# A chunked attention with a token-mixing MLP on one core: mixed product on the full array, small weights on another queue, early casts and a new order of units

## The chip, the core and the metric

The kernel runs on one core of one Trainium2 chip. The metric is the device time of one execution in microseconds (us). Every comparison below is made with runs of the kernel before on the same chip, in the same rounds. A ratio is the mean time of one kernel's fast runs over that of the other's fast runs of the same rounds, so it is not quite the ratio of the medians that are quoted beside it. The span in a profile is some 1.8 us shorter than the time of the same execution.

## The reference

```
attention: q, k, v are [8, 8, 576, 64]; chunks of 64 tokens, no mixing between chunks
  scores = q_c @ k_c.T / 8;  attn = softmax(scores);  out = attn @ v_c
x = heads side by side                       # [8, 576, 512]
wq = x @ w_q;  wk = x @ w_k                  # [8, 576, 64] each
W  = (wq @ wk.T) / 8                         # [8, 576, 576]
out = relu(W @ x) @ w_out                    # [8, 576, 512]
```

Because (wq @ wk.T) @ x = wq @ (wk.T @ x), the kernel never forms W. It computes G = wk.T @ x, 64 x 512 per batch, and then the mixed product wq @ G.

## The kernel before

All work is cut into units and issued in the order of a list, PLAN. TensorE executes its share strictly in the order of the list. The digits are the unit's number and the batch; behind the colon stand the PSUM banks (the tile `banks`, into which TensorE writes).

- `Tq0b`, `Tk0b` (the first 6 of 9 row groups) and `Tq1b`, `Tk1b` (the other 3): VectorE transposes queries and keys.
- `S0b` (double) and `S2b` (single): scores on TensorE, exponentials on ScalarE.
- `Ahb`: attend for two heads on TensorE, normalization (0.21 + 0.82 us) on VectorE.
- `Xnb`: transposes of the result on TensorE, a copy on VectorE.
- `Qb`, `Kb`, `Gb`: projections, transposed key projection, G, each with a copy on ScalarE.
- `Mnb`: mixed product, relu on ScalarE. `O`, `P`: one or two output tiles. An output tile needs only old data, so it is the filler of the order.

```
PLAN = """
Tq00 Tk00 S00:02 Tk10 Tq10 A00:4 S20:0 Tq01 A30:2 Tk01 A20:0 A10:4 S01:62 Tk11 X00:0
X10:2 A01:4 Tq11 A11:0 Q0:2 S21:4 X01:0 Tq02 K0:6 A21:2 G0:0 M00:4 Tk02 A31:0 M10:2
M20:6 S02:42 Tq12 M30:6 X11:0 O:4 Q1:2 Tk12 O:0 ...            (cut)
"""
    load(0)
    make_identity(nc, ident[:])
    for n, w in enumerate((moe_w_q, moe_w_k)):
        for u in range(2):
            nc.gpsimd.dma_start(wraw[...], w...)              # float32 in memory, float16 in SBUF
    for b in range(1, VB):
        load(b)                                                # all loads on the GpSimd queue
...
    def mlp_w(b, a):                                           # Q; in batch 0 it casts wqk first
        ...                                                    # wq in partitions 0-63, wk in 64-127
        nc.scalar.copy(wT[b % 2][:, 0:S]..., a[:, :, 0:HS])
        nc.scalar.copy(wq2[b % 2][CH:, :]..., a[0:CH, :, 0:HS])   # wq again, in partitions 64-127
    def mlp_g(b, a):
        ...
        nc.scalar.copy(g16[b % 2][:], a[:, 0 : DM // 2])       # half of G in each 64 partitions
    def mix(b, n, a):
        i, half = n % 2, n // 2
        for h in range(2):                                     # K = 64: two row halves of the array
            nc.tensor.matmul(a[:, h, 0:HS],
                lhsT=g16[b % 2][CH * h : CH * h + CH, i * P : i * P + P],
                rhs=(wT, wq2)[h][b % 2][CH * h : CH * h + CH, half * HS : half * HS + HS], ...)
        nc.scalar.activation(..., AF.Relu, scale=scale_moe)
```

The softmax here doesn't subtract the row's maximum and nothing guards it: scores larger than these inputs give would overflow.

Of the kernel before, what the change touches and what calls it, by code (L numbers as in the profile page):

```python
# [10 lines left out]
F16 = mybir.dt.float16  # L11
F32 = mybir.dt.float32
# [3 lines left out]
PSUM = bass.MemoryType.PSUM  # L16

PLAN = """
Tq00 Tk00 S00:02 Tk10 Tq10 A00:4 S20:0 Tq01 A30:2 Tk01 A20:0 A10:4 S01:62 Tk11 X00:0
X10:2 A01:4 Tq11 A11:0 Q0:2 S21:4 X01:0 Tq02 K0:6 A21:2 G0:0 M00:4 Tk02 A31:0 M10:2  # L20
M20:6 S02:42 Tq12 M30:6 X11:0 O:4 Q1:2 Tk12 O:0 A02:6 K1:1 S22:4 A12:2 G1:0 M01:6 M11:4
M21:2 Tq03 Tk03 P:0 X02:4 Tk13 S03:26 A22:0 O:4 Tq13 A32:2 O:5 A03:0 M31:6 X12:2 A13:4
S23:6 Q2:0 Tq04 A23:2 O:4 K2:5 Tk04 O:6 A33:0 G2:2 S04:46 Tk14 X03:2 X13:0 O:4 Tq14
A04:2 M02:6 M12:0 Q3:4 A14:6 S24:0 Tq05 K3:2 O:3 M22:4 M32:0 A24:6 G3:2 Tk05 O:3 A34:0
M03:4 O:2 S05:46 Tq15 Tk15 X04:0 O:2 X14:4 M13:6 M23:0 S25:2 A05:4 M33:6 Q4:0 A25:2
A35:4 O:6 Tq06 K4:0 Tk06 Tq16 P:2 O:0 G4:1 A15:2 S06:46 X15:0 O:2 M04:4 Tk16 M14:0 X05:6
A06:2 S26:4 A16:0 O:6 A36:2 M24:4 M34:0 Q5:6 Tq07 X06:2 O:0 K5:1 Tk07 O:4 A26:2 Tq17
Tk17 G5:0 S07:64 O:1 X16:2 S27:6 M05:4 M15:0 Q6:2 A37:6 A27:4 O:0 K6:1 O:6 A17:2 G6:0
A07:4 M25:6 M35:0 X17:2 M06:6 X07:4 M16:0 M26:2 O:6 Q7:0 O:2 O:3 K7:0 O:1 M36:4 G7:2 O:0
M07:4 M17:1 M27:6 O:3 M37:4 O:0 O:1 O:2 O:0 O:1 O:2  # L30
"""


# [1 line left out]
def kernel(  # L35
# [10 lines left out]
    nc = tc.nc  # L46
    B, H, S, D = q.shape
    DM = moe_w_out.shape[0]
    DH = moe_w_q.shape[1]
    P = 128  # L50
# [21 lines left out]
    def each(n, shape, dt, name):  # L72
        return [sb.tile(shape, dt, name=f"{name}{i}") for i in range(n)]
# [2 lines left out]
    kn = each(B, [P, NT, R * D], F16, "kn")  # L76
    vt = each(VB, [P, NP, W], F16, "vt")
    wqk = sb.tile([P, NI, 2 * DH], F16, name="wqk")
    wraw = sb.tile([P, 2, NI, DH], F16, name="wraw")
    wout = sb.tile([P, NI, DM], F16, name="wout")  # L80
    ident = sb.tile([P, P], F16, name="ident")
    zero = sb.tile([P, 512], F16, name="zero")
# [7 lines left out]
    xt = [each(2, [P, S], F32, f"xt{i}_") for i in range(2)]  # L90
    identw = sb.tile([P, P], F32, name="identw")
    wT = each(2, [P, NJ * P], F16, "wT")
    wq2 = each(2, [P, S], F16, "wq2")
    wkn = each(2, [P, NJ, DH], F16, "wkn")
    g16 = each(2, [P, DM // 2], F16, "g16")
    rmx = each(2, [P, NI, 2 * S], F16, "rmx")
    spare = each(2, [P, 2 * DM], F32, "spare")
    mark = sb.tile([1, 2], F16, name="mark")
# [52 lines left out]
        clear_v(i, i > 0)  # L151
    load(0)
    make_identity(nc, ident[:])
    for n, w in enumerate((moe_w_q, moe_w_k)):
        for u in range(2):
            nc.gpsimd.dma_start(
                wraw[CH * u : CH * u + CH, n].rearrange("p (h e) j -> p h (e j)", e=2),
                w.rearrange("(u h p e) j -> u p h (e j)", u=2, h=2, e=2)[u],
            )
# [2 lines left out]

    for i in range(2):
        nc.vector.memset(wT[i][:, S:], 0.0)
    nc.vector.memset(padl[:], 1.0 / P)
    nc.vector.memset(padr[:], 0.0)
    nc.vector.memset(padr[:, 2 * D :], 1.0)
# [30 lines left out]
    def scores(b, s, slots):  # L198
        for t in range(TS):
            for ch in range(2):  # L200
                for e in range(2):
                    for n, a in enumerate(slots):
                        for i in range(2):
                            for u in range(2):
                                h = CH * (u ^ (s + n > 0))
                                o = (2 * t + ch) * CH
                                x = (b, TS * (s + n) + t, 2 * u + i, ch, e)
                                nc.tensor.matmul(  # L208
                                    a[h : h + CH, i, o : o + CH],
                                    lhsT=k_of(*x),  # L210
                                    rhs=q_of(*x),
                                    start=(e == 0),
                                    stop=(e == 1),
                                )
        for n, a in enumerate(slots):
            nc.scalar.activation(  # L216
                est[b % 2][s + n].rearrange("p i t c -> p i (t c)"),
                a[:, :, 0 : 2 * TS * CH],
                AF.Exp,
                scale=scale_attn,  # L220
            )

    def attend(b, h, a):
        af = a.rearrange("p i c -> p (i c)")
# [26 lines left out]

    def xtr(b, n, a):
        tx = a.rearrange("p i c -> p (i c)")
        if "ident" not in done:
            done["ident"] = 1
            nc.scalar.copy(identw[:], ident[:])  # L256
        for j in range(NJ):
            nc.tensor.transpose(  # L258
                tx[:, j * P : j * P + P],
                xn[b % 2].bitcast(F32)[:, j, n * P : n * P + P],  # L260
                identw[:],
            )
        nc.vector.tensor_copy(xt[b % 2][n][:], tx[:, 0:S])  # L263

    def mlp_w(b, a):
        if b == 0:
            nc.scalar.copy(
                wqk.rearrange("p i (n j) -> p n i j", n=2),
                wraw[:],
            )  # L270
        for i in range(NI):
            for h in range(2):
                nc.tensor.matmul(  # L273
                    a[:, h, 0:HS],
                    lhsT=wqk[:, i, :],
                    rhs=xt[b % 2][i // 2]
                    .bitcast(F16)
                    .rearrange("p (s e) -> p s e", e=2)[:, h * HS : h * HS + HS, i % 2],
                    start=(i == 0),
                    stop=(i == NI - 1),  # L280
                )
        nc.scalar.copy(  # L282
            wT[b % 2][:, 0:S].rearrange("p (h n) -> p h n", h=2), a[:, :, 0:HS]
        )
        nc.scalar.copy(
            wq2[b % 2][CH:, :].rearrange("p (h n) -> p h n", h=2), a[0:CH, :, 0:HS]
        )

    def mlp_k(b, a):
# [13 lines left out]
    def mlp_g(b, a):  # L303
        for j in range(NJ):
            for h in range(2):
                nc.tensor.matmul(  # L306
                    a[CH * h : CH * h + CH, 0 : DM // 2],
                    lhsT=wkn[b % 2][:, j, :],
                    rhs=xn[b % 2][:, j, h * 256 : h * 256 + 256],
                    start=(j == 0),  # L310
                    stop=(j == NJ - 1),
                )
        nc.scalar.copy(g16[b % 2][:], a[:, 0 : DM // 2])

    done = {"out": 0, "home": 0}

    def mix(b, n, a):
        i, half = n % 2, n // 2
        for h in range(2):
            nc.tensor.matmul(  # L320
                a[:, h, 0:HS],
                lhsT=g16[b % 2][CH * h : CH * h + CH, i * P : i * P + P],
                rhs=(wT, wq2)[h][b % 2][CH * h : CH * h + CH, half * HS : half * HS + HS],
                start=True,
                stop=True,
            )
        o = (b % 2) * S + half * HS
        nc.scalar.activation(  # L328
            rmx[(b // 2) % 2].rearrange("p (h i) n -> p i h n", h=2)[:, i, :, o : o + HS],
            a[:, :, 0:HS],  # L330
            AF.Relu,
            scale=scale_moe,
        )
# [99 lines left out]
```

## Time and profile before

| | before |
|---|---|
| time, median of 4 runs | 125.7 us (125.18 to 126.4) |
| span of the profile | 125.8 us (of a slow run, 127.58 us) |
| TensorE, VectorE, ScalarE busy | 100.6, 76.2, 81.9 us |
| granted TensorE clock, mean | 0.919 |

Three groups of the profile's view by lines that the change touches follow. The columns are line, engine, operation, output<-input, shapes and count; then busy us and mean ns of one; then the engine's idle time just before them, and what ended most of it.

```profile
L320 PE MATMUL banks<-wq,g 64*128 64x288 f16 x32 | 7.4, 290 | 0.0
...
L285 ACT CAST wq<-banks 64x576 f16<-64x576 f32 x8 | 5.0, 630 | 0.2
...
L313 ACT CAST g<-banks 128x256 f16<-128x256 f32 x8 | 3.0, 379 | 2.3 <-PE banks L306 2.1
```

The change takes the middle group away and doubles the last one in number.

### The profile page before, as it was taken

Reading aid. Unit: us, or ns where it says so; the run is one execution under the profiler, and the core shown is the slowest. Engines: PE = TensorE matmul, PEld = TensorE weight load, DVE = VectorE, ACT = ScalarE, POOL = GpSimd, SP = SyncE. Lnnn points to the kernel's source line nnn. Section 1 sums busy time; section 2 is a strip of 40 time slices with the busy share of each in tenths; the row PEclk is TensorE's granted clock in tenths of the full one; section 3 lists DMA queues with packets and bytes.
Section 4 is the critical chain, followed back from the end, with each engine's and each line's share of the span. In section 5 each row is a group of like instructions: output and inputs, shape, how many; then the busy total and the mean of one; then the engine's idle time right before and its main releaser. Section 6 shows DMA issues by size and latency. Waiting matters only on the chain. (4 is left out here: it accounts for less than half of the span.)

```text
span 125.8 us, 4598 instructions
## 1 busy us (share of the span) xinstructions
PE 100.6 (80%) x1958; PEld 61.5 (49%) x1958; DVE 76.2 (61%) x138; ACT 81.9 (65%) x137; POOL 72.0 (57%) x107
## 2 busy tenths in 40 slices
PE   6923450399779789989599979999999896999970
PEld 2303450385455645656556556565667564544420
DVE  5538319847794397979477955895999266400000
ACT  7992500512668777665569858668696795788960
POOL 6989889972798579579769948976400000000000
PEclk9996555556999999999999999999999999999999
DMA  1999999999999999999999999999999999936494
GB/s 13 161 172 160 140 172 176 150 145 196 195 163 170 190 158 139 175 190 153 160 190 162 155 183 181 129 168 186 167 214 386 366 348 382 376 122 244 167 352 150
DMA packets 63113, 24.55 MB, mean 195 GB/s; under 512 B 39540, under 2 KB 58484, under 8 KB 63092
## 3 DMA queue, kind: packets, MB, share of 16 engines
q0 software_dynamic: 57936, 14.82, 128.3%
q1 hardware_dynamic: 5156, 9.44, 20.2%
q8 instruction: 15, 0.25, 0.8%
q14 instruction: 6, 0.05, 0.1%
HBM read 29.62 MB, written 9.44 MB: 310 GB/s over the span
## 5 line engine op out<-in xcount | busy, mean ns | idle before, releaser
L341 PE MATMUL banks<-wout,rmx 128*128 128x512 f16 x144 | 35.7, 380 | 0.8 <-issue 0.8
L216 ACT ACTIVATE est<-banks 128x768 f16<-128x768 f32 x24 | 18.7, 809 | 19.1 <-PE banks L208 19.1
L118 POOL DMA_DIRECT2D vt<-in_v_dram x32 | 27.3, 859 | 6.0 <-DMA kn<-in_k_dram 1.7
L244 DVE TENSOR_TENSOR xn<-banks,rec 128x640 f16<-128x640 f32 x32 | 26.4, 824 | 1.1
L107 POOL DMA_DIRECT2D kn<-in_k_dram x32 | 20.9, 666 | 10.3 <-DMA vt<-in_v_dram 8.2
L208 PE MATMUL banks<-qT,kT 32*64 32x64 f16 x1152 | 14.6, 218 | 11.6 <-DVE rec L243 5.3
L107 POOL DMA_DIRECT2D qn<-in_q_dram x32 | 21.0, 680 | 1.0 <-POOLq L417 0.8
L328 ACT ACTIVATE rmx<-banks 128x576 f16<-128x576 f32 x32 | 19.5, 656 | 2.9 <-PE banks L320 2.6
L181 DVE STREAM_TRANSPOSE kT<-kn 128x768 f32<-128x768 f32 (+1 forms) x16 | 19.4, 1213 | 2.3 <-DMA kn<-in_k_dram 2.2
L208 PEld LDWEIGHTS <-kT 32*64 32x64 f16 x1152 | 12.1, 112 | 15.8 <-DVE rec L243 6.7
L341 PEld LDWEIGHTS <-rmx 128*128 128x128 f16 x144 | 12.5, 98 | 12.9 <-issue 1.1
L234 PE MATMUL banks<-vt,est 128*64 128x130 f16 x288 | 16.0, 241 | 3.4 <-DMA vt<-in_v_dram 2.4
L263 DVE COPY xt<-banks 128x576 f32<-128x576 f32 x16 | 12.0, 756 | 10.9 <-PE banks L258 9.2
L234 PEld LDWEIGHTS <-est 128*64 128x64 f16 x288 | 11.4, 120 | 9.9 <-issue 5.3
L181 DVE STREAM_TRANSPOSE qT<-qn 128x768 f32<-128x768 f32 (+1 forms) x16 | 12.4, 773 | 5.1 <-DMA qn<-in_q_dram 5.0
L258 PE MATMUL banks<-identw,xn 128*128 128x128 f32 x80 | 12.6, 298 | 3.4 <-ACT identw L256 1.8
L243 DVE RECIPROCAL rec<-banks 128x10 f32<-128x10 f32 x32 | 6.6, 206 | 11.5 <-PE banks L234 5.9
L258 PEld LDWEIGHTS banks<-identw,xn 128*128 128x128 f32 x80 | 9.7, 151 | 6.2 <-ACT identw L256 1.9
L359 ACT COPY qn<-banks 128x512 f32<-128x512 f32 x16 | 9.4, 590 | 4.6 <-PE banks L341 4.4
L359 ACT COPY kn<-banks 128x512 f32<-128x512 f32 (+1 forms) x15 | 9.2, 624 | 3.6 <-PE banks L341 3.2
L273 PE MATMUL banks<-xt,wqk 128*128 128x288 f16 x64 | 10.4, 309 | 0.0
L282 ACT CAST wT<-banks 128x576 f16<-128x576 f32 x8 | 5.1, 641 | 6.7 <-DVE xn L244 5.2
(36 smaller groups left out, 88.5 us busy)
## 6 DMA issues: line engine op xcount, KB each, us to landing
out_dram<-qn SPq DMA_DIRECT2D x16, 256.0 KB, 4.0
out_dram<-kn SPq DMA_DIRECT2D x14, 256.0 KB, 3.9
qn<-in_q_dram POOLq DMA_DIRECT2D x16, 192.0 KB, 6.1
kn<-in_k_dram POOLq DMA_DIRECT2D x16, 192.0 KB, 7.0
vt<-in_v_dram POOLq DMA_DIRECT2D x16, 192.0 KB, 6.2
qn<-in_q_dram POOLq DMA_DIRECT2D x16, 96.0 KB, 7.1
kn<-in_k_dram POOLq DMA_DIRECT2D x16, 96.0 KB, 5.6
vt<-in_v_dram POOLq DMA_DIRECT2D x16, 96.0 KB, 5.5
```

The source lines that it names most:

```text
L107: nc.gpsimd.dma_start(dst[b][CH * u : CH * u + CH, a:e, :], src[b] .rearrange("h s d -> (h s) d") .rearrange("(u t p r) d -> u p t (r d)", ...
L118: nc.gpsimd.dma_start(vt[b % VB][h : h + CH, a:e, D * u : D * u + D], v[b] .rearrange("h s d -> (h s) d") .rearrange("(u g p) d -> u p g d ...
L181: nc.vector.transpose(out=o, in_=src[b].bitcast(F32)[:, a:e, :].rearrange("p t (r d) -> p t r d", d=32),)
L208: nc.tensor.matmul(a[h : h + CH, i, o : o + CH], lhsT=k_of(*x), rhs=q_of(*x), start=(e == 0), stop=(e == 1),)
L216: nc.scalar.activation(est[b % 2][s + n].rearrange("p i t c -> p i (t c)"), a[:, :, 0 : 2 * TS * CH], AF.Exp, scale=scale_attn,)
L234: nc.tensor.matmul(af[CH * (c % 2) : CH * (c % 2) + CH, o : o + W], lhsT=lhsT, rhs=rhs, start=True, stop=True,)
L244: nc.vector.tensor_tensor(out=xn[b % 2] .rearrange("p j (a u b d) -> p j a u b d", a=2, u=2, b=2)[:, :, h // 2, :, h % 2, :], in0=xv[:, :, ...
L258: nc.tensor.transpose(tx[:, j * P : j * P + P], xn[b % 2].bitcast(F32)[:, j, n * P : n * P + P], identw[:],)
L263: nc.vector.tensor_copy(xt[b % 2][n][:], tx[:, 0:S])
L328: nc.scalar.activation(rmx[(b // 2) % 2].rearrange("p (h i) n -> p i h n", h=2)[:, i, :, o : o + HS], a[:, :, 0:HS], AF.Relu, scale=scale_moe,
L341: nc.tensor.matmul(a[:, x, :], lhsT=rmx[pr % 2][:, i, tl * P : tl * P + P], rhs=wout[:, 2 * (i % 2) + i // 2, :], start=(i == 0), stop=(i ...
L359: nc.scalar.copy(os_, a[:, 0:w, :])
```

## The change

G is kept whole in 64 partitions and padded with zeros to 128, so that the mixed product uses the full array and needs no second copy of wq. The small weights leave the GpSimd queue, so that batch 1 can be issued sooner. The casts move forward into idle time of ScalarE. The order of units is new, with S0 and S2 of a batch further apart.

```diff
 PLAN = """
-Tq00 Tk00 S00:02 Tk10 Tq10 A00:4 S20:0 Tq01 A30:2 Tk01 A20:0 A10:4 S01:62 Tk11 X00:0
-X10:2 A01:4 Tq11 A11:0 Q0:2 S21:4 X01:0 Tq02 K0:6 A21:2 G0:0 M00:4 Tk02 A31:0 M10:2
-M20:6 S02:42 ...                                                     (cut)
+Tk00 Tq00 Tq10 Tk10 Tq01 S00:02 S20:4 Tk01 A30:0 S01:24 A20:0 A00:6 Tk11 A10:2 X10:4
+Tq11 A11:0 A01:2 S21:4 X00:0 A31:2 Tq02 Tk02 Q0:4 A21:0 K0:2 Tq12 X01:4 S02:62 X11:0
+G0:6 ...                                                             (cut)
-    wraw = sb.tile([P, 2, NI, DH], F16, name="wraw")
+    wraw = sb.tile([P, 2, NI, DH], F32, name="wraw")
-    g16 = each(2, [P, DM // 2], F16, "g16")
+    g16 = each(2, [P, DM], F16, "g16")                # rows 64-127 are set to zero once
+    nc.sync.dma_start(mark[:], kn[0][P - 1 : P, 0, 0:2])   # waits for the first keys
-            nc.gpsimd.dma_start(wraw ...
+            nc.sync.dma_start(wraw ...
     def scores(b, s, slots):  ...
+        if b == 0 and s == 0:                          # both casts, taken out of X and Q
+            nc.scalar.copy(identw[:], ident[:])
+            nc.scalar.copy(wqk..., wraw[:])
-        nc.scalar.copy(wq2[b % 2][CH:, :]..., a[0:CH, :, 0:HS])
-        nc.scalar.copy(g16[b % 2][:], a[:, 0 : DM // 2])
+        for h in range(2):
+            nc.scalar.copy(g16[b % 2][0:CH, h * 256 : h * 256 + 256], a[CH * h : CH * h + CH, 0 : DM // 2])
-                lhsT=g16[b % 2][CH * h : CH * h + CH, i * P : i * P + P],
-                rhs=(wT, wq2)[h][b % 2][CH * h : CH * h + CH, half * HS : half * HS + HS],
+                lhsT=g16[b % 2][:, h * 256 + i * P : h * 256 + i * P + P],
+                rhs=wT[b % 2][:, half * HS : half * HS + HS],
```

More of the change, by code (lines that the diff above doesn't have):

```diff
@@ L18 @@
 PLAN = """
-Tq00 Tk00 S00:02 Tk10 Tq10 A00:4 S20:0 Tq01 A30:2 Tk01 A20:0 A10:4 S01:62 Tk11 X00:0
-X10:2 A01:4 Tq11 A11:0 Q0:2 S21:4 X01:0 Tq02 K0:6 A21:2 G0:0 M00:4 Tk02 A31:0 M10:2
-M20:6 S02:42 Tq12 M30:6 X11:0 O:4 Q1:2 Tk12 O:0 A02:6 K1:1 S22:4 A12:2 G1:0 M01:6 M11:4
-M21:2 Tq03 Tk03 P:0 X02:4 Tk13 S03:26 A22:0 O:4 Tq13 A32:2 O:5 A03:0 M31:6 X12:2 A13:4
-S23:6 Q2:0 Tq04 A23:2 O:4 K2:5 Tk04 O:6 A33:0 G2:2 S04:46 Tk14 X03:2 X13:0 O:4 Tq14
-A04:2 M02:6 M12:0 Q3:4 A14:6 S24:0 Tq05 K3:2 O:3 M22:4 M32:0 A24:6 G3:2 Tk05 O:3 A34:0
-M03:4 O:2 S05:46 Tq15 Tk15 X04:0 O:2 X14:4 M13:6 M23:0 S25:2 A05:4 M33:6 Q4:0 A25:2
-A35:4 O:6 Tq06 K4:0 Tk06 Tq16 P:2 O:0 G4:1 A15:2 S06:46 X15:0 O:2 M04:4 Tk16 M14:0 X05:6
-A06:2 S26:4 A16:0 O:6 A36:2 M24:4 M34:0 Q5:6 Tq07 X06:2 O:0 K5:1 Tk07 O:4 A26:2 Tq17
-Tk17 G5:0 S07:64 O:1 X16:2 S27:6 M05:4 M15:0 Q6:2 A37:6 A27:4 O:0 K6:1 O:6 A17:2 G6:0
-A07:4 M25:6 M35:0 X17:2 M06:6 X07:4 M16:0 M26:2 O:6 Q7:0 O:2 O:3 K7:0 O:1 M36:4 G7:2 O:0
-M07:4 M17:1 M27:6 O:3 M37:4 O:0 O:1 O:2 O:0 O:1 O:2
+Tk00 Tq00 Tq10 Tk10 Tq01 S00:02 S20:4 Tk01 A30:0 S01:24 A20:0 A00:6 Tk11 A10:2 X10:4
+Tq11 A11:0 A01:2 S21:4 X00:0 A31:2 Tq02 Tk02 Q0:4 A21:0 K0:2 Tq12 X01:4 S02:62 X11:0
+G0:6 Tk12 A02:4 Q1:2 M00:0 S22:6 M10:4 K1:2 A12:0 A32:6 A22:4 G1:0 Tk03 Tq03 O:1 M20:6
+M30:2 M01:4 M11:0 O:6 X12:2 X02:4 Tq13 S03:06 O:2 Tk13 Q2:4 A03:0 S23:6 A13:4 K2:2 M21:0
+M31:6 O:3 Tq04 G2:0 A33:4 A23:6 O:1 M02:2 Tk04 M12:4 Tq14 O:0 M22:6 O:1 Tk14 M32:2 X13:4
+X03:6 S24:0 S04:24 Q3:6 O:0 A24:2 A14:4 A34:6 K3:1 O:0 O:1 Tq05 Tq15 G3:2 A04:4 O:0 O:1
+M03:6 Tk15 M13:4 Tk05 X14:2 M23:0 X04:6 O:4 M33:0 S25:2 S05:64 Tq06 Q4:0 P:2 A25:0 A15:4
+K4:6 O:7 A05:0 G4:2 A35:4 O:3 Tk16 X05:0 M04:4 O:2 Tq16 M14:6 X15:4 S26:0 Tk06 M24:2
+Q5:6 A36:0 S06:24 Tq07 O:6 K5:0 Tk07 M34:2 O:1 A06:4 A16:6 G5:0 A26:2 O:1 M05:4 O:0
+X06:6 M15:2 Tk17 S07:40 X16:6 O:2 M25:4 Q6:6 Tq17 S27:0 A17:4 A07:6 K6:2 O:3 M35:0 A27:4
+G6:2 A37:6 O:3 X07:0 M06:4 X17:6 O:2 M16:0 Q7:4 O:2 K7:0 M26:4 O:1 G7:0 M36:4 O:1 M07:6
+M17:2 O:0 M27:4 M37:6 O:1 O:0 O:2 O:1 O:0 O:2
 """
@@ L92 @@
     wT = each(2, [P, NJ * P], F16, "wT")
-    wq2 = each(2, [P, S], F16, "wq2")
     wkn = each(2, [P, NJ, DH], F16, "wkn")
-    g16 = each(2, [P, DM // 2], F16, "g16")
+    g16 = each(2, [P, DM], F16, "g16")
     rmx = each(2, [P, NI, 2 * S], F16, "rmx")
@@ L153 @@
     make_identity(nc, ident[:])
+    nc.sync.dma_start(mark[:], kn[0][P - 1 : P, 0, 0:2])
     for n, w in enumerate((moe_w_q, moe_w_k)):
         for u in range(2):
-            nc.gpsimd.dma_start(
+            nc.sync.dma_start(
                 wraw[CH * u : CH * u + CH, n].rearrange("p (h e) j -> p h (e j)", e=2),
@@ L164 @@
         nc.vector.memset(wT[i][:, S:], 0.0)
+        nc.vector.memset(g16[i][CH:, :], 0.0)
     nc.vector.memset(padl[:], 1.0 / P)
@@ L221, in scores @@
             )
+        if b == 0 and s == 0:
+            nc.scalar.copy(identw[:], ident[:])
+            nc.scalar.copy(
+                wqk.rearrange("p i (n j) -> p n i j", n=2),
+                wraw[:],
+            )
     def attend(b, h, a):
@@ L253, in xtr @@
         tx = a.rearrange("p i c -> p (i c)")
-        if "ident" not in done:
-            done["ident"] = 1
-            nc.scalar.copy(identw[:], ident[:])
         for j in range(NJ):
@@ L265, in mlp_w @@
     def mlp_w(b, a):
-        if b == 0:
-            nc.scalar.copy(
-                wqk.rearrange("p i (n j) -> p n i j", n=2),
-                wraw[:],
-            )
         for i in range(NI):
@@ L283, in mlp_w @@
             wT[b % 2][:, 0:S].rearrange("p (h n) -> p h n", h=2), a[:, :, 0:HS]
-        )
-        nc.scalar.copy(
-            wq2[b % 2][CH:, :].rearrange("p (h n) -> p h n", h=2), a[0:CH, :, 0:HS]
         )
@@ L312, in mlp_g @@
                 )
-        nc.scalar.copy(g16[b % 2][:], a[:, 0 : DM // 2])
+        for h in range(2):
+            nc.scalar.copy(
+                g16[b % 2][0:CH, h * 256 : h * 256 + 256],
+                a[CH * h : CH * h + CH, 0 : DM // 2],
+            )
     done = {"out": 0, "home": 0}
```

## The prediction

> **What bounds the kernel now.** I began with the busy table by stretches of time, because one average over the span mixes a start that waits with an end that is full. Its columns are the stretch and its length, then busy us (with instruction counts) of PE, PEld, DVE, ACT and POOL, the granted clock, the DMA share and GB/s.
>
> ```profile
> 11.00:25.00 14.00, 5.44 (x280) 4.68 (x280) 8.30 (x13) 4.04 (x7) 13.26 (x21) 0.50 1.82 159
> 25.00:30.00 5.00, 4.96 (x36) 3.90 (x37) 3.15 (x7) 0.50 (x1) 2.86 (x5) 0.50 1.51 163
> 30.00:36.30 6.30, 4.57 (x97) 2.85 (x95) 4.87 (x7) 4.30 (x8) 4.51 (x6) 0.94 1.59 188
> 36.30:47.60 11.30, 10.12 (x225) 6.55 (x226) 7.28 (x10) 8.38 (x15) 8.60 (x13) 1.00 1.86 169
> ...
> 95.40:109.10 13.70, 12.07 (x254) 7.70 (x253) 8.18 (x14) 10.00 (x18) 0.00 (x0) 1.00 1.00 370
> 109.10:122.00 12.90, 12.76 (x78) 5.74 (x76) 0.00 (x0) 10.93 (x22) 0.00 (x0) 1.00 0.61 229
> ```
>
> There are three regimes. Up to about 30 us TensorE is mostly idle and at half clock. From 36 to 109 it is busy some 90% of the time. In the last 13 us it is full. So the end is set by when TensorE gets going, by what it has to do, and by the holes in between. Loads end near 90 us and don't set the end: the last batch's first query part was issued at 79.36 and its transpose ran at 91.74 without a wait for data.
>
> Next the timeline of the start (start, duration, engine, what, and in brackets the idle time before it and what ended it):
>
> ```profile
> 18.55 0.98 DVE L181 STREAM_TRANSPOSE qT<-qn 128x768 f32<-128x768 f32 x1 [3.48 <-DMA qn<-in_q_dram]
> ...
> 20.62 1.53 DVE L181 STREAM_TRANSPOSE kT<-kn 128x768 f32<-128x768 f32 x1
> ...
> 22.20 1.08 PE L208 MATMUL banks<-qT,kT 32*64 32x64 f16 x96 [4.43 <-DVE rec L243]
> ...
> 25.04 2.39 PE L258 MATMUL banks<-identw,xn 128*128 128x128 f32 x10 [1.76 <-ACT identw L256]
> ```
>
> VectorE waited 3.48 us for the queries of batch 1; from 18.55 to 30.7 it then worked with only some 2 us of holes, and TensorE followed it (the 4.43 us wait ends when the key transpose ends at 22.15). The cast of the identity, last in ScalarE's order, held the transposes another 1.76 us. This stretch is bound by that arrival and by VectorE's order.
>
> Last, the mixed product among its neighbours on TensorE (same columns):
>
> ```profile
> 85.73 1.03 PE L341 MATMUL banks<-wout,rmx 128*128 128x512 f16 x4
> 86.69 0.29 PE L320 MATMUL banks<-wT,g 64*128 64x288 f16 x1
> 86.69 0.29 PE L320 MATMUL banks<-wq,g 64*128 64x288 f16 x1
> 86.82 0.28 PE L320 MATMUL banks<-wT,g 64*128 64x288 f16 x1
> 86.82 0.28 PE L320 MATMUL banks<-wq,g 64*128 64x288 f16 x1
> 87.04 0.77 PE L258 MATMUL banks<-identw,xn 128*128 128x128 f32 x5
> ```
>
> The two halves start together, and the next pair comes 0.13 us later: a unit M costs 0.125 us, not 0.25. But the four output matmuls before it need 4 x 0.216 = 0.86 us, and M starts 0.96 us after they did; the last pair takes 0.22 until the transposes start. So about 0.10 us is lost on entering and again on leaving the half-array shape. The same shows at other changes of shape (attend to output at 89.17: 0.10 more than attend to attend), and not between two full-array kinds (output at 108.25, projection at 109.12: 0.87).
>
> **What the Trainium skill says.** "TensorEngine Tiling (Array Packing)", section Key Properties: changing the tiling mode drains TensorE. The trace agrees, at about 0.10 us a change. "TensorE: Matmul & The Clock Gate", Part 3 (packing small matmuls): matmuls in different row groups run concurrently; agrees, both at 86.69. The same page, Part 1: the clock starts at half rate and is released after some 3.4 us of activity; agrees roughly, as the clock is 0.50 from 11 to 30 us and full after the dense stretch from 25 on. "DMA: Bandwidth & Descriptors", Issuing engines are not separate DMA queues: all queues share the same 16 engines, so another queue saves only issue time. No run here shows that yet; the moved weights test it.
>
> **The change part by part.**
>
> *Full-array mix.* Each M goes from 0.125 to 2 x 0.12 = 0.245 us: 32 x 0.12 = +3.84 us of streaming. Against this, M no longer changes the shape next to transposes, projections, key products and outputs. I counted changes of shape along both orders (four kinds: full, 128x64 for A and G, 32x64 for S, 64x128 for the old M): 93 before, 55 after. So -38 x 0.10 = -3.8 us. The full array in the old order would have 71 changes, 3.84 - 2.2 = +1.6 us: the order pays the rest.
>
> TensorE's sum at full clock, from start-to-start distances in the timeline (0.85 a double S, 0.52 a single, 0.31 A, 0.54 X, 1.0 Q, 0.15 K, 0.55 G, 0.865 an output tile): 8x0.85 + 8x0.52 + 32x0.31 + 16x0.54 + 8x1.0 + 8x0.15 + 8x0.55 + 36x0.865 = 74.3. Before: + 32x0.125 + 93x0.10 = 87.6. After: + 32x0.245 + 55x0.10 = 87.6. TensorE's work is unchanged; this surprised me, as the streaming alone looked like a loss.
>
> *ScalarE.* Eight copies into the second half are gone: 8 x 0.630 (row of wq) = -5.0. The copy of G (0.379) becomes two of 64 partitions; halving partitions saved nothing for wq against wT (0.630 against 0.641), so + 8 x 0.38 = +3.0. Net -2.0 us on an engine that is busy 65%: nearly all beside other work. The key copy comes 0.63 sooner and the second half of G 0.38 later, worth 0.25 us where the chain Q-K-G-M has no filler. The output units fill most of it: I count 0.2 us.
>
> *Early casts.* The identity cast (0.30) and weight cast (0.63) move from 24.68 to about 15, when ScalarE is idle. This removes the 1.76 us wait, but VectorE's order is the bound behind it, so I give it no separate credit. The weights are now float32 on the sync queue behind the first keys (landed 9.33); if late, they delay the exponential of S20, for which there are some 3 us of room.
>
> *Weights off the GpSimd queue.* Four issues of 0.60 us go: batch 1 is issued 2.4 us sooner. The transfers still share the engines, busy over 90% from 3 us on, so I expect the queries of batch 1 not 2.4 but about 1 us sooner: 17.5 instead of 18.55.
>
> *Order at the start.* The new order moves attend 0 of batch 0 out of VectorE's idle time (14 to 15 us, 1.04 us) and leaves X01 (0.76) for later. The first keys are transposed before the first queries, so S00 starts after 9.33 + 1.53 + 0.98 = 11.8 instead of 10.9, with no effect, because batch 1 isn't there yet. From Tq01 to Tk02 VectorE has four transposes of b1 (0.98+1.53+0.87+0.57), seven attends (7 x 1.04), two copies (2 x 0.76), Tq02 and Tk02 (0.98+1.55): 15.3 us. From 17.5, with 1.5 to 2 us of holes, S02 starts at about 34.5 to 35 against 36.33, having had 9.2 us of TensorE work before it against 10.3. TensorE's lag behind its own sum thus goes from 26.0 to about 25 to 25.5: a gain of 0.8 us.
>
> *Order in the middle.* The lag before is 26.0 at S02, 31.9 at S07 (95.42 - 63.5), 34.3 at the end (121.88 - 87.6). Of these 8.3 us, some 3.8 are holes inside units (0.65 at 43.1, 0.55 at 56.1, 1.26 at 61.5, 0.75 at 74.8, 0.63 in two others) that wait for no engine; an order can't remove them. About 3 are waits for VectorE or ScalarE (1.24 at 106.27, 0.85 at 36.33, 0.47 at 44.7, 0.42 at 85.16). With S0 and S2 of a batch apart, I expect a third of these back: 1.0 us, a choice rather than a result.
>
> Sum: 0.0 (TensorE) - 0.8 (start) - 1.0 (middle) - 0.2 (chain) = -2.0 us. The tail after TensorE (a copy of 0.58 and the last transfer, 3.9 us together) stays. From 125.5 that is 123.5 us.
>
> **Rivals.** (1) *The full array costs what it streams.* If the 0.10 at a shape change is not really saved, TensorE has +3.8 us; as it is full at the end, the time would be near 127. For it: M is denser in the last third, where nothing hides it. Against it: the gaps around the old M are in every case I looked at.
> (2) *Loads take over.* If batches are started sooner but the engines can't deliver, VectorE waits for each batch and only the last one's slack counts. For it: the DMA row is 9 to slice 34 and loads go at 160 to 170 GB/s. Against it: batches 2 to 6 had 2.8 to 6 us between estimated landing and transpose. It would leave 125 to 126.
> (3) *The order removes most waits*, and the denser start brings the full clock 2 us sooner. Then 3 us of waits and 1 to 2 us at half clock come back: 121 to 122. Against it: some waits always return in another place, and VectorE bounds the start.
>
> **Range and chances.** My sum is 123.5, with rival 3 somewhat likelier than rival 1 because the new order looks made to group full-array work. I put 123.4, with 121.0 to 126.0 as the range. The bound for "faster by over 2%" is 122.98, a little below my number: 0.40. Slower by over 2% (127.98) needs rival 1 in full: 0.05. The rest, 0.55, is within 2%.
>
> **What would show it.** Right: M pairs 0.12 apart, one after another, with the next full-array unit following without a gap; TensorE's busy sum within 2 us of 100.6; Tq01 near 17.5; S02 near 35 and S07 between 93 and 96; ScalarE near 80. Wrong: waits for q or k before the transposes of batches 2 to 7 (rival 2); a last stretch after S07 longer than before's 26.5 us (rival 1); a new wait of ScalarE for the weights near 14 us that delays S20; or a clock that reaches 1.0 well before or after 30 us.

## The result

The changed kernel took 129.73 us in the median of 4 runs (128.49 to 130.09), against 125.7 us before. Executions over 1.5% slower than the fastest of the same kernel are left out of the means. The ratio of the fast runs is 1.0299, with a 95% interval of 1.021 to 1.039: slower by 3%, where 1.7% faster was predicted. Its profile is of a fast run: span 128.3 us, clock 0.894, TensorE, VectorE and ScalarE busy 101.4, 75.7 and 79.3 us. So the work is as predicted and the time isn't.

The busy table by equal stretches tells where the time went. Its columns are the stretch and its length, busy us (with instruction counts) of PE, PEld, DVE, ACT and POOL, the clock, the DMA share and GB/s. First the control, which is the kernel before in a fast run:

```profile
8.00:20.00 12.00, 4.39 (x184) 3.76 (x184) 5.59 (x8) 4.04 (x6) 10.97 (x18) 0.64 1.73 164
20.00:30.00 10.00, 5.85 (x138) 4.61 (x138) 7.67 (x14) 2.21 (x4) 7.52 (x11) 0.58 1.80 165
30.00:40.00 10.00, 7.51 (x201) 5.23 (x201) 6.57 (x11) 6.66 (x11) 7.90 (x12) 0.77 1.79 173
40.00:54.00 14.00, 13.53 (x258) 8.04 (x256) 9.83 (x17) 9.83 (x16) 10.39 (x15) 0.92 1.73 171
```

Then the changed kernel:

```profile
8.00:20.00 12.00, 1.93 (x144) 1.78 (x144) 3.56 (x5) 3.42 (x6) 8.23 (x13) 0.59 1.80 181
20.00:30.00 10.00, 4.18 (x139) 3.66 (x140) 7.01 (x11) 2.84 (x4) 7.91 (x11) 0.50 1.58 150
30.00:40.00 10.00, 7.13 (x123) 5.26 (x125) 8.46 (x14) 1.88 (x3) 6.95 (x10) 0.79 1.71 167
40.00:54.00 14.00, 13.13 (x288) 9.49 (x287) 9.29 (x14) 8.98 (x17) 10.10 (x15) 0.88 1.89 167
```

Idle time of TensorE is the length minus its busy time. It grew by 2.5 us from 8 to 20, by 1.7 us from 20 to 30 and by 0.4 us in each of the next two stretches: 4.9 us in all. TensorE ended at 124.33 instead of 119.59, 4.7 us later. The whole loss lies in idle time of TensorE, and most of that before 30 us. Against the control the clock isn't the cause: half of TensorE's busy time at half clock between 8 and 68 us, read in steps of 1 us, is 7.2 us in the control and 6.7 us in the changed kernel. But the control has a second stretch at half clock, from 35.3 to 42.1 us, that three other traces of the old order lack: the profile on record, e1 and e4 lose 5.6, 5.6 and 5.0 us. Against those, 1.0 to 1.7 us of the changed kernel's loss are clock.

It helps to speak of TensorE's lag: the time at which a unit starts, minus the sum of the work that stands before it in the order (the prediction's durations, with 0.10 us for each change of shape). Starts are read from the timelines, to about 0.2 us.

| lag in us | at S01 | at S02 | at S03 | at S05 | at S07 | end |
|---|---|---|---|---|---|---|
| before, control | 18.9 | 26.3 | 29.1 | 29.7 | 30.3 | 32.0 |
| changed | 21.7 | 30.8 | 34.1 | 34.6 | 35.5 | 36.7 |

The changed kernel loses 4.5 us before S02, 0.5 us up to S03, and gains 0.3 us in the rest. Now its start, in the timeline (start, duration, engine, line, what; in brackets the idle time before it and what ended that):

```profile
19.97 0.98 DVE L182 STREAM_TRANSPOSE qT<-qn 128x768 f32<-128x768 f32 x1 [7.06 <-DMA qn<-in_q_dram]
20.16 0.62 ACT L225 CAST wqk<-wraw 128x512 f16<-128x512 f32 x1 [5.44 <-DMA wraw<-in_moe_w_k_dram]
...
21.54 0.75 PE L241 MATMUL banks<-vt,est 128*64 128x130 f16 x9 [7.71 <-ACT est L217]
...
23.56 1.08 PE L209 MATMUL banks<-qT,kT 32*64 32x64 f16 x96 [1.27 <-DVE rec L250]
...
29.42 1.30 PE L262 MATMUL banks<-identw,xn 128*128 128x128 f32 x5 [3.01 <-DVE xn L251]
...
39.37 0.66 PE L262 MATMUL banks<-identw,xn 128*128 128x128 f32 x4 [1.80 <-DVE xn L251]
```

Four suspects show here. The weights came late, and ScalarE's early cast waited 5.44 us for them, which held the exponential of S20 and with it attend 3 (7.71 us). The queries of batch 1 landed at 19.97 instead of 18.2. VectorE did nothing for 7 us. And X01, in front of S02 on TensorE, waited 1.80 us for a normalization. The longest wait looks like the culprit; the experiments show that it isn't.

### The profile page after: what moved, and what is told of

Same layout as the page of the kernel before. It is cut to its first block, busy times and chain, and to the rows that moved or that the text cites.

```text
span 128.3 us, 4610 instructions
## 1 busy us (share of the span) xinstructions
PE 101.4 (79%) x1958; PEld 66.4 (52%) x1958; DVE 75.7 (59%) x140; ACT 79.3 (62%) x138; POOL 69.7 (54%) x103
## 3 DMA queue, kind: packets, MB, share of 16 engines
q0 software_dynamic: 57360, 14.69, 123.5%
## 4 chain that ended last, share of the span: by engine, by line
PE 47%; DMA 19%; DVE 12%; POOL 7%; issue 7%; ACT 6%; DVEq 0%; ACTq 0%; POOLq 0%
PE banks L341 17%; DMA kn<-in_k_dram 12%; DVE xn L251 7%; PE banks L262 7%; DMA qn<-in_q_dram 6%; PE banks L320 6%; PE banks L209 5%; PE banks L272 4%; PE banks L241 4%; PE banks L302 3%; POOL vt L117 3%; POOL qn L106 3%; ACT est L217 2%; DVE qT L182 2%; DVE rec L250 2%
## 5 line engine op out<-in xcount | busy, mean ns | idle before, releaser
L217 ACT ACTIVATE est<-banks 128x768 f16<-128x768 f32 x24 | 18.5, 809 | 20.2 <-PE banks L209 19.9
L182 DVE STREAM_TRANSPOSE kT<-kn 128x768 f32<-128x768 f32 (+1 forms) x16 | 19.1, 1202 | 4.3 <-DMA kn<-in_k_dram 4.3
L328 ACT ACTIVATE rmx<-banks 128x576 f16<-128x576 f32 x32 | 20.2, 665 | 2.1 <-PE banks L320 2.0
L241 PE MATMUL banks<-vt,est 128*64 128x130 f16 x288 | 15.1, 242 | 7.7 <-ACT est L217 7.7
L341 PEld LDWEIGHTS <-rmx 128*128 128x128 f16 x144 | 13.2, 98 | 12.2 <-issue 0.5
L209 PE MATMUL banks<-qT,kT 32*64 32x64 f16 x1152 | 13.7, 219 | 6.2 <-DVE qT L182 4.8
L262 PE MATMUL banks<-identw,xn 128*128 128x128 f32 x80 | 13.6, 304 | 5.8 <-DVE xn L251 5.7
L262 PEld LDWEIGHTS banks<-identw,xn 128*128 128x128 f32 x80 | 10.2, 154 | 8.0 <-DVE xn L251 4.0
L320 PE MATMUL banks<-wT,g 128*128 128x288 f16 x64 | 12.2, 286 | 0.2 <-DVE xn L251 0.2
L272 PE MATMUL banks<-xt,wqk 128*128 128x288 f16 x64 | 9.7, 294 | 0.4 <-DVE xt L267 0.4
```

Of the source, the lines that this page charges most:

```text
L182: nc.vector.transpose(out=o, in_=src[b].bitcast(F32)[:, a:e, :].rearrange("p t (r d) -> p t r d", d=32),)
L209: nc.tensor.matmul(a[h : h + CH, i, o : o + CH], lhsT=k_of(*x), rhs=q_of(*x), start=(e == 0), stop=(e == 1),)
L217: nc.scalar.activation(est[b % 2][s + n].rearrange("p i t c -> p i (t c)"), a[:, :, 0 : 2 * TS * CH], AF.Exp, scale=scale_attn,)
L241: nc.tensor.matmul(af[CH * (c % 2) : CH * (c % 2) + CH, o : o + W], lhsT=lhsT, rhs=rhs, start=True, stop=True,)
L262: nc.tensor.transpose(tx[:, j * P : j * P + P], xn[b % 2].bitcast(F32)[:, j, n * P : n * P + P], identw[:],)
L320: nc.tensor.matmul(a[:, h, 0:HS], lhsT=g16[b % 2][:, h * 256 + i * P : h * 256 + i * P + P], rhs=wT[b % 2][:, half * HS : half * HS + HS], ...
```

## The experiments

Eighteen kernels ran; all gave the right result. The control says how finely ratios can be read. In the call of e13 to e16 one run of the kernel before is unusually short (122.84 us), so only 3 of its 12 runs count as fast. The ratios of this call are therefore high against the others: the ratios of the medians are 1.026, 1.030, 1.028 and 1.045.

| run | what it is | ratio to before (95%) |
|---|---|---|
| e1_mix_only | before + full-array mix | 1.001 (0.997 to 1.005) |
| e2_order_only | before + new order | 1.046 (1.037 to 1.055) |
| e3_casts_late | changed, casts as before | 1.033 (1.022 to 1.044) |
| e4_old_order | changed, old order | 1.004 (0.998 to 1.009) |
| e5_before_again | control | 0.992 (0.987 to 0.997) |
| e6_old_head | e2, old order up to S02 | 1.021 (1.008 to 1.034) |
| e7_new_head | before, new order up to S02 | 1.059 (1.049 to 1.069) |
| e8_free_attends | e2, four attends moved forward | 1.027 (1.013 to 1.040) |
| e9_fillers | e6, output tiles moved forward | 1.040 (1.025 to 1.055) |
| e10_old_head_s01 | e2, old order up to S01 | 1.038 (1.028 to 1.048) |
| e11_weights_pool | changed, weights on GpSimd | 1.022 (1.013 to 1.031) |
| e12_best_guess | e1 + early cast of the identity | none (too few fast runs) |
| e13_swap | changed, Tq02 and Tk02 moved back | 1.041 (1.026 to 1.055) |
| e14_swap_old_s01 | e10 with the same swap | 1.041 (1.011 to 1.070) |
| e15_old_s03_full | e1, new order after S03 | 1.049 (1.038 to 1.060) |
| e16_old_s03_half | before, new order after S03 | 1.066 (1.051 to 1.082) |
| e17_old_s05_full | e1, new order after S05 | 1.010 (1.006 to 1.014) |
| e18_new_head_s01 | before, new order up to S01 | 1.033 (1.027 to 1.040) |

**Taking the change apart.** My theory after reading the two traces was that the late weights cost the time, through ScalarE's wait or through late loads; the rival was the order.

e1: the parts of the diff for `g16`, `wq2` and `mix` alone.

```diff
-rhs=(wT, wq2)[h]... lhsT=g16[half of the partitions]
+rhs=wT...           lhsT=g16[all partitions, zero-padded]
```

> The kernel before with the full-array mixed product and nothing else (old order, weights on GpSimd, late casts). Theory 'shape changes pay' (mine): TensorE +3.84 us of streaming, 22 fewer shape changes -2.2 us, the removed copies of wq worth a few tenths: +1 to +1.6 us, ratio to before 1.008 to 1.013. Rival 'the full array costs what it streams': +3 to +4 us, ratio 1.024 to 1.032, that is the whole loss. M pairs 0.12 us apart in both.

Measured: 125.96 us against 125.28, ratio 1.001. The full array costs nothing, less than my +1 to +1.6 us. The rival (+3 to +4 us) falls.

e2: the new PLAN alone.

```diff
-PLAN = old
+PLAN = new
```

> The kernel before with the new order and nothing else (half-array mix, weights on GpSimd, late casts). Theory 'weights': the queries of batch 1 land near 18.5 us again, S02 starts at 37 to 38 instead of 40.0, and the time is 125 to 126.5 us, ratio 0.995 to 1.01. Rival 'order': the order itself starves TensorE between 20 and 50 us, so the time stays at 128 us or above, ratio at least 1.02.

Measured: 130.65 us, ratio 1.046. The queries of batch 1 were back at 18.32, S02 started at 37.9, and yet the lag was 28.8 at S02 and 33.2 at S03. The order alone loses at least as much as the whole change. My theory falls.

e3: the casts put back into X and Q, the weights still on the sync queue.

```diff
-        if b == 0 and s == 0:   # casts behind S00
+    (identity cast in the first X, weight cast in Q0)
```

> The changed kernel with both casts put back where they were (weights still on the sync queue, new order, full array). Theory 'stall' : ScalarE's 5.4 us wait for the weights delays S20 and with it attend 3, TensorE's 7.7 us wait; without it the time falls by 2.5 us or more, to 127 or below. Rival 'late loads': attend 3 is hidden behind the transposes of batch 1, which wait for loads; the 5.4 us wait goes but the time stays within 0.7 us of the changed kernel (ratio to before 1.024 to 1.036).

Measured: 129.2 us, ratio 1.033, the same as the changed kernel within the intervals. The stall is gone from the timeline, and nothing follows from it:

```profile
16.26 0.72 PE L235 MATMUL banks<-vt,est 128*64 128x130 f16 x9 [2.56 <-DMA vt<-in_v_dram]
...
23.51 1.07 PE L209 MATMUL banks<-qT,kT 32*64 32x64 f16 x96 [6.49 <-DVE rec L244]
```

Attend 3 runs at 16.26 instead of 21.54, and the next unit, S01, starts at 23.51 instead of 23.56, because it waits for the keys of batch 1. A wait of 7.7 us cost nothing, as another one ended later.

e4: the changed kernel with the old PLAN.

```diff
-PLAN = new
+PLAN = old
```

> The changed kernel in the old order (full array, weights on sync, early casts). Theory 'weights and casts': the same 5.4 us wait of ScalarE appears, and in the old order the normalization of attend 3 stands in front of the key transposes of batch 1, so the loss is as large or larger: 128 us or more. Rival 'order': without the new order the loss goes, 125.5 to 127 us.

Measured: 126.11 us, ratio 1.004. With the old order, all the rest of the change together is neutral. The rival, the order, is right. The trace adds a point: ScalarE waits 5.45 us for the weights here too, the first query transpose starts at 19.09, and S01 starts at 23.66, as late as in the changed kernel. Yet S02 starts at 36.24, a little before the control's 36.58. So a late S01 isn't the loss either.

**The control.** e5 is the kernel before, unchanged.

> The kernel before, unchanged, as a control, because its profile on record fell in a slow run. Ratio 1.000 within 0.006; a profile of a fast run with a span about 2 us shorter (some 123.7 us), the score units of batch 7 starting near 93.5 instead of 95.4, and fewer of the holes inside units on TensorE (below 2 us instead of 3.8). If the holes are the same and the span is 125.8 again, the profile on record was typical.

Measured: 125.43 us against 126.35 of the same kernel, ratio 0.992 (0.987 to 0.997), outside the expected 0.6%. So one kernel differs from itself by 0.8%, and differences of less than about 1% aren't read as effects here. Span 123.5 us, as expected, and TensorE idled only 0.27 us between 54 and 80.

**Where in the order.** e6 and e7 splice the two orders at S02 (weights on GpSimd, late casts, half-array mix, as in e2).

```diff
-PLAN = new                      # e6
+PLAN = old up to S02, then the units that are left in the new order
-PLAN = old                      # e7
+PLAN = new up to S02, then the units that are left in the old order
```

> Order-only kernel (ratio 1.046) with the old order up to and with the double score unit of batch 2 (S02), then the rest in the new order. Theory 'head': the first 36 us, in which VectorE stands idle behind the transposes of batch 1, are the loss; ratio 1.00 to 1.015 and a lag of about 26 at S02. Rival 'tail': the new order's middle, without output units as fillers until batch 1 is mixed, is the loss; ratio 1.025 or more although the lag at S02 is 26.

> The mirror: the new order up to S02, then the old order's rest. Theory 'head': ratio 1.025 or more. Rival 'tail': ratio 1.01 or less, as the old rest fills the holes. If both halves lose some 0.02 each, both theories hold in part.

Measured: 1.021 and 1.059. In e6 the lag is 26.3 at S02, as in the control, and 31.3 at S03; in e7 it is 30.5 and 36.9. Neither half is free. A splice also makes its own neighbours, which e7 shows: its lag jumps by 6 us from S02 to S22, a pair of units that neither order has with the same things between.

e8 moves four attends of batch 0, with their normalizations, in front of the first units of batch 1.

```diff
-Tk00 Tq00 Tq10 Tk10 Tq01 S00:02 S20:4 Tk01 A30:0 S01:24 A20:0 A00:6 Tk11 A10:2 X10:4
+Tk00 Tq00 Tq10 Tk10 S00:02 S20:4 A30:0 A20:0 A00:6 A10:2 Tq01 Tk01 S01:24 Tk11 X10:4
```

> Order-only kernel with one local move: attends 3, 2, 0 and 1 of batch 0 stand before the first transposes and score unit of batch 1, so that their four normalizations (4.2 us of VectorE) run while it waits for the loads. Theory 'in-order VectorE': S02 starts 2.5 to 3.5 us sooner than in the order-only kernel (37.9) and at least 2 us of that reaches the end, ratio 1.02 to 1.03. Rival 'no filler': the time gained at S02 is lost again by S03, because the chain X-Q-K-G-M of batches 0 and 1 has nothing beside it; ratio stays above 1.035.

Measured: 1.027, against 1.046 for the order alone. The direction and the final ratio are as expected. The path isn't: S02 started at 38.5, not sooner. Attend 3, first in the line, got its values only at 15.77, while the old order starts with attend 0, whose values were there at 13.04; so VectorE waited 3.74 us, the four normalizations ended at 21.8, and the transposes of batch 1 stood behind them.

e9 moves output tiles forward in e6, between S02 and S03.

```diff
-S02:42 Tq12 X11:0 Tk12 A02:4 Q1:2 S22:6 K1:2 A12:0 ... O:1 M30:2 ... O:6 ... O:2 ... O:3
+S02:42 Tq12 M30:6 X11:0 O:7 Tk12 A02:4 Q1:2 O:0 S22:6 K1:2 O:1 A12:0 A32:6 A22:4 O:3 ...
```

> The old-head kernel (1.021, lag 26.3 at S02, 31.3 at S03) with the last mix of batch 0 and four output tiles moved forward to stand between S02 and S03, where the new order has none; nothing else. Theory 'no filler': TensorE's holes between S02 and S03 are only waits of one chain and fill up; the lag at S03 falls to 29 or 29.5, the time by 1.5 us or more, ratio 1.00 to 1.01. Rival 'chain': the chain itself is late, the tiles delay it by what they take (4 x 0.865 = 3.5 us), the lag at S03 stays near 31 and the ratio near 1.02.

Measured: 1.040 from two fast runs, worse than e6 (1.021) and outside both expectations. The lag at S03 was 32.8. A lack of fillers between S02 and S03 isn't what can be mended by hand there.

e10 splices at S01 instead of S02; e11 is the changed kernel with the weights on GpSimd.

```diff
-PLAN = new                      # e10
+PLAN = old up to S01, then the units that are left in the new order
-    nc.sync.dma_start(mark...); nc.sync.dma_start(wraw...)     # e11
+    nc.gpsimd.dma_start(wraw...)                               # float16 again
```

> Order-only kernel with the old order up to and with S01 only, then the new rest. Theory 'first 22 us': everything that the head loses is the missing attend 0 at 13 us and the transposes in front of the normalizations, so S02 is back at a lag of 26 to 27 (order only 28.8). Rival 'S01 to S02': the new order there, with X01 in front of S02 on TensorE and behind Tk02 on VectorE, loses 1.5 us or more by itself, and the lag at S02 stays at 27.5 to 29 although S01 is at 19 to 20. In both the middle loses as in the old-head kernel: ratio 1.025 to 1.04.

> The changed kernel with the weights back on the GpSimd queue as float16 (early casts, new order and full array kept). Theory 'weights delay the loads': the first query transpose of batch 1 is back at 18.3 to 18.6 us (changed: 19.97), S01 at 22 (23.6), and the time falls by 0.8 to 1.6 us, ratio 1.018 to 1.025. Rival: start and time don't follow each other, as the middle loses it again; ratio 1.028 or more.

Measured: e10 1.038, with S01 at 23.2 and a lag of 29.8 at S02. The lag grows by 9.6 us from S01 to S02, in the control by 7.4: the new order between S01 and S02 loses by itself, as its rival said. X01 waited 2.66 us there. e11 1.022: that ratio is the one that the theory expected, but the first query transpose was at 18.93 and S01 at 22.98, later than expected, and S02 was at 39.5 instead of 40.0. The intervals of e11 and the changed kernel overlap, so late weights may be up to about 1 us of the loss, or nothing.

e12 tried for a kernel better than before.

```diff
+        if b == 0 and s == 0:            # e1, and:
+            nc.scalar.copy(identw[:], ident[:])
```

> The old order with the full-array mix, weights on GpSimd, and of the early casts only the identity's (its input is there at 11 us). Theory 'identity cast': TensorE's 1.76 us wait before the first transposes goes, of which up to 1 us is real because the last normalization ends at 23.7; ratio to before 0.990 to 0.998, ratio to the mix-only kernel (1.0008) -0.3 to -1%. Rival: VectorE bounds the start anyway, ratio 0.998 to 1.004.

Measured: 126.39 us against 126.33, with too few fast runs for a ratio. No gain is to be seen.

**The crossed queues.** In the new order X01 stands in front of S02 on TensorE and waits for the normalization of A21, which stands behind Tq02 and Tk02 on VectorE. e13 (changed kernel) and e14 (e10) turn this round.

```diff
-A31:2 Tq02 Tk02 Q0:4 A21:0 K0:2 Tq12 X01:4 S02:62
+A31:2 Q0:4 A21:0 K0:2 Tq02 Tk02 Tq12 X01:4 S02:62
```

> The changed kernel with one swap: the query and key transposes of batch 2 stand behind Q0, A21 and K0 instead of in front of them, on VectorE behind the normalization of A21. Theory 'crossed queues': X01 in front of S02 on TensorE waits for a normalization that stands behind Tk02 on VectorE; with the swap its 1.8 us wait goes, S02 starts 1 to 1.5 us sooner (changed 40.0) and the ratio falls by 0.007 to 0.012, to about 1.018 to 1.023. Rival: it only moves the wait, as VectorE has the same work in front of S02: S02 within 0.5 us and the ratio unchanged (1.026 or more).

> The old-head-to-S01 kernel (1.038, X01 waits 2.66 us at 38.3, S02 at 39.2) with the same swap. Theory 'crossed queues': S02 at 37 to 37.8, ratio 1.02 to 1.03. Rival: no change, 1.035 or more.

Measured: 1.041 and 1.041; no gain. The timeline of e13 tells why:

```profile
36.98 0.66 PE L262 MATMUL banks<-identw,xn 128*128 128x128 f32 x4 [0.42 <-DVE xn L251]
...
39.29 1.08 PE L209 MATMUL banks<-qT,kT 32*64 32x64 f16 x96 [1.65 <-DVE kT L182]
```

X01 waits 0.42 us instead of 1.80, and S02 now waits 1.65 us for the key transpose. The wait moved from one unit to the next, since VectorE has the same work in front of S02 either way. S02 came 0.7 us sooner, a little more than the rival's 0.5, and the ratio didn't fall: the rival is right in the main. (The profile of e14 fell in a slow run and isn't read.)

X01 waits for A21, but it doesn't read what A21 writes. By the code, `X0b` reads the first 256 columns of `xn`, which A0 and A1 fill, and A2 and A3 fill the others. The changed kernel's trace shows the split:

```profile
30.82 0.76 DVE L267 COPY xt<-banks 128x576 f32<-128x576 f32 x1 [1.55 <-PE banks L262]
...
36.94 1.50 DVE L182 STREAM_TRANSPOSE kT<-kn 128x768 f32<-128x768 f32 x1
...
37.26 0.31 PE L262 MATMUL banks<-identw,xn 128*128 128x128 f32 x1
...
38.49 0.82 DVE L251 TENSOR_TENSOR xn<-banks,rec 128x640 f16<-128x640 f32 x1
...
39.96 0.98 PE L209 MATMUL banks<-qT,kT 32*64 32x64 f16 x96
```

The first of X01's five transposes ran at 37.26; the other four ran at 39.37, after A21's normalization. In the built program the second transpose waits for the count that VectorE reaches with that normalization, and X10 waits likewise for A10's, though it reads only what A20 and A30 write (this is the wait of 3.01 us at 29.42). The old order has neither wait at the start, as X01 stands before A21 there and X00, which needs A10, before X10. Without them S02 could start when Tk02 ends, at 38.44, and VectorE's 1.55 us wait for X10 would go too: an estimate of up to 3 us from these lines. An order with X01 in front of A21 and X10 in front of A00 and A10 wasn't tried, so how much of the order's loss is these two waits stays open.

**Is the rest of the new order neutral?** e15, e16 and e17 keep the old order further.

```diff
-PLAN = old                      # e15 full array, e16 half array; e17 with S05 for S03, full array
+PLAN = old up to S03, then the units that are left in the new order
```

> Old order up to and with S03, then the new order; full-array mix, weights on GpSimd, late casts (so the mix-only kernel with a new tail). Theory 'all of the loss lies before S03': lag at S03 about 27.2 as in mix only, then +2.5 to the end as in the changed kernel, and TensorE's sum is 87.8 instead of 89.2: end at 117.5, span 121.4 against 122.9, ratio 0.985 to 0.993. Rival 'the new tail loses too, or shape changes aren't worth what I counted': 1.00 to 1.01.

> The same order with the half-array mix (so the kernel before with a new tail). TensorE's sum 87.8 by my count, as before. Theory 'all of the loss lies before S03': ratio 0.997 to 1.005, and the full mix is better here by 0.8 to 1.5%. Rival 'new tail loses': 1.01 or more.

Measured: 1.049 and 1.066. In e15 both expectations failed; e16 falls under its rival (1.01 or more). In e15 the lag is 27.1 at S03, as in e1 (27.2), and 32.9 at S23, six units of TensorE later. The splice had taken out the output tiles there, and left a bare chain of attend, transpose and projection:

```profile
50.60 0.44 PE L234 MATMUL banks<-vt,est 128*64 128x130 f16 x9 [1.65 <-ACT est L216]
...
53.29 1.33 PE L258 MATMUL banks<-identw,xn 128*128 128x128 f32 x5 [1.93 <-DVE xn L244]
```

In the second of these two holes, at 51.7 us, the clock fell to half, and it stayed there to 58.5. This tells nothing on the new order; it shows what one place without fillers costs.

> Old order up to and with S05 (about 71 us), then the new order; full-array mix, weights on GpSimd, late casts. Sum of TensorE's work 88.9 against 89.2 in the mix-only kernel. Theory 'the new order loses only early': lag at S05 28.1 as in mix only, growth to the end 1.7 to 2.5 us, ratio 0.995 to 1.006. Rival 'it loses everywhere, later only more slowly': lag growth from S05 to the end of 3.5 us or more, ratio 1.012 or more.

Measured: 126.73 us against 125.32, ratio 1.010, between the two expectations. With output tiles on both sides of the splice, the new order after S05 may cost about 1% against e1 (1.001), which is no more than the control differs from itself. Its profile fell in a slow run, so where isn't told.

**The start alone.** e18 puts only the new order's units up to S01 into the kernel before.

```diff
-Tq00 Tk00 S00:02 Tk10 Tq10 A00:4 S20:0 Tq01 A30:2 Tk01 A20:0 A10:4 S01:62 Tk11 X00:0 ...
+Tk00 Tq00 Tq10 Tk10 Tq01 S00:02 S20:4 Tk01 A30:0 S01:24 A00:4 A20:0 A10:4 Tk11 X00:0 ...
```

> The kernel before (half mix, weights on GpSimd, late casts) with the new order up to S01, then the old one. Theory 'VectorE in front of S02': attend 0 of batch 0 is normalized behind Tk01 instead of at 14 us, which puts 1.04 us more work of VectorE in front of S02; S02 1 us later than in the control (36.7), half to all of it at the end: ratio 1.004 to 1.012. Rival 'the loss is in the first 22 us': ratio 1.02 or more. Rival 'it is hidden': 1.00.

Measured: 129.22 us, ratio 1.033: the rival's value. In the control four attends run while TensorE waits for batch 1 (start, duration, engine, what; the last line is S02):

```profile
13.04 0.72 PE L234 MATMUL banks<-vt,est 128*64 128x130 f16 x9 [1.22 <-DMA vt<-in_v_dram]
...
15.58 0.72 PE L234 MATMUL banks<-vt,est 128*64 128x130 f16 x9 [1.01 <-ACT est L216]
...
16.09 0.75 PE L234 MATMUL banks<-vt,est 128*64 128x130 f16 x9
...
16.63 0.75 PE L234 MATMUL banks<-vt,est 128*64 128x130 f16 x9
...
36.58 1.08 PE L208 MATMUL banks<-qT,kT 32*64 32x64 f16 x96 [0.93 <-DVE rec L243]
```

In e18 only one does, at 16.35, and the others stand behind S01 (first line; the last is S02):

```profile
22.09 1.07 PE L208 MATMUL banks<-qT,kT 32*64 32x64 f16 x96 [4.99 <-DVE rec L243]
...
24.73 0.70 PE L234 MATMUL banks<-vt,est 128*64 128x130 f16 x9 [1.57 <-ACT est L216]
...
25.59 0.22 DVE L243 RECIPROCAL rec<-banks 128x10 f32<-128x10 f32 x1 [2.67 <-PE banks L234]
...
39.63 0.98 PE L208 MATMUL banks<-qT,kT 32*64 32x64 f16 x96 [0.70 <-DVE rec L243]
```

S01 starts at nearly the same time in both (21.91 in the control). But in the control VectorE goes from the key transpose straight to products that already lie in PSUM. In e18 it waits 2.67 us for the first of them, whose bank S01 still holds. The last normalization of batch 0 ends at 28.8 instead of 23.7, S02 starts at 39.6 instead of 36.6, and that runs through to the end. Part of this is the splice's own: its A00 takes bank 4, one of S01's, and waits 1.57 us for S01's exponential. In e2, which has the same order up to S01, the next attend takes bank 0 and starts at 22.95 without a wait, VectorE waits 0.97 us, and S02 starts at 37.9. So the 1.033 isn't the price of the start alone.

## Why the prediction was wrong

The step that failed is "Order at the start", which promised that the lag at S02 goes "from 26.0 to about 25 to 25.5: a gain of 0.8 us". It went to 30.8, against 26.3 in the control. The terms of that step:

- "17.5 instead of 18.55" for the queries of batch 1: measured 19.97, so 2.5 us late. Issued 2.3 us sooner they landed later, next to weights on another queue. In the four traces with the weights on the sync queue the transpose starts at 19.1 to 20.1; in those with them on GpSimd at 18.2 to 18.9, but once at 19.6 (e10; e8, where it was moved, isn't counted). e4 and e11 show that little of this reaches the end.
- "seven attends": eight. I read S02 as waiting for Tk02, but X01 stands in front of it on TensorE and waits for A21, whose result it doesn't read. That is 1.0 us more for VectorE.
- "1.5 to 2 us of holes": 3.9 us of waits for loads and for TensorE between 19.97 and 39.3; 1.55 us of them wait for X10, which TensorE held for a result that it doesn't read. VectorE needs something to do; the step counted its work as if its inputs lay ready. In the old order they do, because the attends of batch 0 ran in the wait before S01. In e4 three of them run as late as 20.2 to 21.8, but still in front of S01, and nothing is lost. In the new order they stand behind S01. e18 shows the move at 1.033, with a bank clash of its own in it.

These add up to about the 5.5 us between my 34.5 and the measured 40.0. I had seen the single moved normalization ("out of VectorE's idle time"); I hadn't asked which TensorE work had been filling the same wait.

What held, and what else the prediction said:

- "TensorE's work is unchanged" holds in the trace of the changed kernel. The columns are those of the timeline above:

```profile
116.28 1.03 PE L341 MATMUL banks<-wout,rmx 128*128 128x512 f16 x4
117.14 0.65 PE L320 MATMUL banks<-wT,g 128*128 128x288 f16 x4
117.63 1.03 PE L341 MATMUL banks<-wout,rmx 128*128 128x512 f16 x4
```

The four output matmuls hand over after 0.86 us without a gap, and the four matmuls of two M units take 0.49 us, 0.12 each. TensorE's busy sum is 101.4 instead of 100.6. From S07 to the end the changed kernel needs 24.2 us, the control 25.9 (it has 1.1 us more work left there), and e1 has 1.001, so rival 1 is out. For the full array in the old order I had counted +1.6 us; e1 shows none of it in the time, and its lag at the end is 2.2 us smaller than the control's. Of these 2.2 us, 1.6 are clock (7.2 us lost at half clock in the control, 5.6 in e1); the rest isn't explained.
- "Net -2.0 us" for ScalarE: measured -2.6 in busy time (81.9 to 79.3), beside other work, as said.
- "Early casts" were given no credit; rightly. The sign that I had named for being wrong, "a new wait of ScalarE for the weights", came, and was not the cause. I had allowed "some 3 us of room" before a late cast harms; it was late by 5.4 us and harmed nothing (e3).
- "Order in the middle", 1.0 us back: measured from S02 to the end 5.9 us of lag growth against 5.8 in the control (3.6 in e1), so nothing came back. Of the "3.8 us of holes inside units", the control has only a small part (0.3 us): they belonged largely to the slow run that I took for typical. Its bracket "slow" stood beside the profile, and I didn't look.

What stays open: how much the new order between S01 and S03 costs by itself. Each splice there lost 2 us or more, but splices make their own holes (e7, e15). That the order as a whole costs the time is shown (e2, e4). That the start costs by leaving the attends behind S01 is read from traces and fits e18, but e18 has a bank clash in it. How much is due to X10 and X01 waiting for results that they don't read wasn't tested; a sum over the parts isn't shown either. No kernel that I ran beats the one before by more than the control's scatter.

## What to carry to other kernels

When a start is bound by loads, list for every engine the work whose inputs are already there during the wait, and check that no unit of the next batch stands in front of it in any engine's order. Judge a long wait by what waits next: here 7.7 us cost nothing, and moving the wait of one unit only gave it to the next. Ask of a wait whether the unit reads what it waits for; here two units didn't. When an order is changed, test the order by itself first, and look at the state of the run whose profile is read.

## What the Trainium skill lacked or had wrong

- "TensorEngine Tiling (Array Packing)", Key Properties, says that a change of mode drains TensorE, without a size. Here a change between half and full array costs about 0.10 us on entering and 0.10 us on leaving (0.96 instead of 0.86 us from output to M before, 0.86 after).
- "TensorE: Matmul & The Clock Gate", in its table of rules, warns of idle gaps of more than about 3 us (elsewhere the page tells of shorter ones that do it too, without a size). In e15 the clock fell to half at 51.7 us, in the second of two holes of 1.65 and 1.93 us with attends between them. In the control it fell at 35.3 us, though no hole of TensorE in the 3 us before was longer than 0.63 us.
- "DMA: Bandwidth & Descriptors", Issuing engines are not separate DMA queues, says that another queue saves only issue time. Here the weights on the sync queue, as float32, landed 6.4 to 7.7 us after their issue; on GpSimd, as float16, 3.9 to 5.0 us in the kernel before and 5.0 to 5.4 us in e11. Queue and type changed together, so this doesn't tell which of the two it was, and it doesn't contradict the page.
